# The first layer's bias of a fused attention and gated MLP block: loaded as 14 rows and turned on TensorE instead of by single elements

## The chip, the cores and the metric

One core of a Trainium2 chip runs the kernel. The metric is the device time of one execution in microseconds, of which the median of several runs is taken. Each engine (TensorE or PE, VectorE or DVE, ScalarE or ACT, GpSimd or POOL, and SyncE or SP, which issues the DMAs) works through its own list of instructions in a fixed order.

## What is computed

```python
# x: (1, 2048, 512); 32 query heads of 16, one shared key and value head of 16
xn = _layernorm(x)
q, k, v = xn @ wq, xn @ wk, xn @ wv
s = softmax(q k^T / 4) v  (each head), joined, @ wo
h = xn @ w1 + b1                       # w1: (512, 1792), b1: (1792,)
act = h * tanh(softplus(h))            # Mish
g = silu(act @ w2)                     # w2: (1792, 512)
return x + s * g
```

All inputs and the result are in 32 bits.

## The kernel before

The sequence is cut into four chunks of 512 rows (`C`), the model width into four tiles of 128, and the hidden width of 1792 into `NFT` = 14 tiles of 128. Attention works in 32 units, one for each chunk and group of four heads; a unit is 16 steps of 128 keys. Most products split both operands into a high part (fp32r) and a low part and add three partial products, so for the projection of one weight tile on one chunk TensorE runs 12 matmuls of 128x512 (`mm12`, L649; `Mm`, L104).

Three streams are interleaved on TensorE. Products `m` (L1073) give scores whose row maxima DVE takes (L1077). Products `e` (L1044) give the scores again, turned, with the maximum taken off by two more rows of the operands; ACT takes their exponential (L1049), and `pv` (L1131) multiplies it by the values. All projections (q, both MLP layers, the output) run as groups `xps` in the gaps between (`fill`, `waves`, `unit`).

The kernel is unrolled in full by Python code. In the main part the order on each engine is set by patterns and due times. In the lead-in, some first 90 us, a small planner sets it (the loop at L1428): it keeps a list of tasks for each engine with assumed durations and writes the task that can start first. What stands before that loop (L1284 to L1300) is written out in the order of the code, ahead of every planned instruction of its engine.

The lead-in runs so. SP issues the loads of x in tiles of 128 rows (`load_x`, L221), with the first weight tile of q (`load("wq")`), both tiny weight matrices `wk` and `wv` and the first tile of w1 (`load("ws")`, tile `rawws`) between. TensorE runs 24 products on a zeroed tile (`warm`, L1299). For the first chunk DVE takes the statistics of four tiles (L239, L240) and `ve` (L258); ACT makes `rstd` from it with Ln and Exp (L261, L262), DVE refines it and makes `nbias` (L255), ACT and DVE scale the rows (L211, L287), TensorE turns them (`xp`, L298), ACT copies the high part to `xt` (L307) and DVE the low part (L169). Then follow the first group of q (`xps`, L112), the keys and values (`kp`, L339), the copies `qh`/`ql` and their moves into the query tiles `qt` by DMA (L741), and the first maxima `m`. The same steps follow for chunks 1 to 3, in part on POOL (L287, L273 to L282). TensorE gets extra products on zeros (`keep_warm`, L1384) where the planner sees a gap.

The bias b1 is needed with one hidden column on each partition: `b1c`, 128 partitions x 14, is the bias operand of the ACT instruction that ends each group of the first MLP layer:

```python
bias = b1c[:, ft:ft + 1]
act.activation(hb, ps, AF.Identity, bias=bias)      # L785, the first at 56.5 us
```

Its load is the one line

```python
sp.dma_start(b1c, b1.rearrange("(t p) -> p t", p=P))   # L1292
```

which stands in SP's list behind eight tiles of x, the first tiles of wq and w1, wk and wv, and ahead of the other eight tiles of x. Neighbours in a row of `b1c` lie 512 bytes apart in DRAM, so each of the 1792 elements is a piece of its own of four bytes.

Each engine's list is strict: what waits holds all that stands behind it. The DMAs that SP issues share one set of queues on the 16 DMA engines, and eight completion semaphores are used in turn, so that SP issues a DMA only when the one eight places before has landed.

Of the kernel before, what the change touches and what calls it, by code (L numbers as in the profile page):

```python
# [14 lines left out]
F32 = mybir.dt.float32  # L15
F32R = mybir.dt.float32r
AF = mybir.ActivationFunctionType
# [3 lines left out]
P = 128  # L21
# [9 lines left out]
NFT = F // P  # L31
# [91 lines left out]
def block_kernel(ctx: ExitStack, tc: tile.TileContext, x, wq, wk, wv, wo, w1, b1, w2, out):  # L123
    nc = tc.nc
    cp = ctx.enter_context(tc.tile_pool(name="const", bufs=1))
    sb = ctx.enter_context(tc.tile_pool(name="work", bufs=2))
    ps_e = ctx.enter_context(tc.tile_pool(name="ps_e", bufs=3, space=bass.MemoryType.PSUM))
    ps_m = ctx.enter_context(tc.tile_pool(name="ps_m", bufs=3, space=bass.MemoryType.PSUM))
    ps_v = ctx.enter_context(tc.tile_pool(name="ps_v", bufs=1, space=bass.MemoryType.PSUM))
# [4 lines left out]
    pe, act, dve, pool, sp = nc.tensor, nc.scalar, nc.vector, nc.gpsimd, nc.sync  # L134
# [51 lines left out]
    ident = cp.tile([P, P], F32, name="ident")  # L186
# [15 lines left out]
    b1c = cp.tile([P, NFT], F32, name="b1c")  # L202
# [12 lines left out]
    def new_xt(c):  # L215
        xt_of[c] = sb.tile([P, 2, NDT, C], F32R, tag="xt", name=f"xt{c}", bufs=2)
        return xt_of[c]
# [3 lines left out]
    def load_x(c):  # L221
        for tt in range(4):
            if 4 * c + tt < NPT:
                xin[c, tt] = pts[:, 4 * c + tt]
            else:
                xin[c, tt] = sb.tile([P, D], F32, tag=("y0", "sc")[tt % 2], name=f"xin{c}_{tt}", bufs=1)
            sp.dma_start(xin[c, tt], xr[4 * c + tt])
            if (c, tt) == (1, 0):
                sp.dma_start(wkv[:, 0], wk.rearrange("(t p) n -> p t n", p=P))
                sp.dma_start(wkv[:, 1], wv.rearrange("(t p) n -> p t n", p=P))  # L230
                wk_split()
# [213 lines left out]
    def arrived(tag):  # L445
        k, n = todo[tag]
        if taken(tag, k) or tag == "ws" and k < 12 and k > posted[0] + (4 if lead and now[0] < 50 else 2):
            return False
        return k < n and items[tag][k].step + 1 <= (step[0] if lead else max(step[0], step_of(busy[0])) + 0.3)
# [45 lines left out]
    def load(tag):  # L495
        its = items[tag]
        k, n = todo[tag]
        if tag == "wx" and m1_done.get((NC - 2, NFT - 1)) is None or lead and tag == "wq" and n > 1:
            return
        if n == len(its):  # L500
            return
        it = its[n]
        if taken(tag, n) and (tag != "ws" or kept.get(it.key)):
            return
        if n == k and kept.get(it.key):
            it.tile = home(tag, n)
            sp.dma_start(f(it.tile), kept[it.key])
            it.ready = math.ceil(2 * (sp_at(0.5) + 1.6)) / 2
            todo[tag][:] = n + 1, n + 1
        elif n - k < NRAW[tag] and freed and freed[0] <= step[0] + (0.1 if lead else 0.8):  # L510
            freed.popleft()
            r = sb.tile([P, D], F32, tag="raw", name=f"raw{tag}{n}", bufs=RAWS)
            if len(it.src.shape) == 3:
                sp.dma_start(r.rearrange("p (t n) -> p t n", t=NDT), it.src)
            else:
                sp.dma_start(r, it.src)
            it.raw, it.step = r, (lead["arrive"]() if lead else sp_at(0.45))
            todo[tag][1] += 1
# [770 lines left out]
    load_x(1)  # L1289
    xat.update({t: landed(DMA_US) for t in range(4, 8)})  # L1290
    load("ws")
    sp.dma_start(b1c, b1.rearrange("(t p) -> p t", p=P))  # L1292
    load_x(2)
    load_x(3)
    xat.update({t: landed(DMA_US) for t in range(8, 16)})
# [1 line left out]
    warm = ps_v.tile([P, C], F32, tag="v", name="warm")  # L1297
    for _ in range(NWARM):
        pe.matmul(warm, qts[0][:, 0, 0:P], qts[0][:, 0], start=True, stop=True)  # L1299
    new_xt(0)  # L1300
    used = {"e": [], "v": []}

# [117 lines left out]
    def soon(k, t):  # L1420

        return all(d.end is not None and d.end < t + 2.0 or d.end is None and d.deps and d.eng != "DVE" and all(x.end is not None for x in d.deps)
                   for d in k.deps)
# [4 lines left out]
    while True:  # L1428
# [59 lines left out]
        elif k == "J":  # L1488
            tag = next((g for g in ("wq", "ws", "wb") if not any(soon(k, s) for k in plan["POOL"]) and arrived(g) and busy[0] + E0 < s + (4.5 if g == "ws" else 0.5)), None)
# [194 lines left out]
```

## Time and profile before

| | |
|---|---|
| median of 3 runs | 1571.32 us (1570.73 to 1571.49) |
| the profiled execution's own time | 1572.05 us |
| its span (first to last instruction) | 1570.3 us |
| outside the span | 1.75 us |
| mean granted TensorE clock | 0.997 |
| busy: PE, DVE, ACT, POOL | 1556.2, 1348.8, 1289.8, 635.7 us |
| DMA | 73863 packets, 125.47 MB |

The profile is of one execution. A row of its timeline has the start and the duration in us, the engine, the line, the operation, the tiles written and read, and in brackets how long the engine sat idle before it and what released it. A row by stretches has, for each engine, its busy time and in brackets its instructions, then the granted TensorE clock, the share of the 16 DMA engines that was busy, and GB/s. PE is TensorE's matmuls, PEld its weight loads, SPq a DMA issued by SP.

### The profile page before, as it was taken

Reading aid. Unit: us, or ns where it says so; the run is one execution under the profiler, and the core shown is the slowest. Engines: PE = TensorE matmul, PEld = TensorE weight load, DVE = VectorE, ACT = ScalarE, POOL = GpSimd, SP = SyncE. Lnnn points to the kernel's source line nnn. Section 1 sums busy time; section 2 is a strip of 40 time slices with the busy share of each in tenths; the row PEclk is TensorE's granted clock in tenths of the full one; section 3 lists DMA queues with packets and bytes.
Section 4 is the critical chain, followed back from the end, with each engine's and each line's share of the span. In section 5 each row is a group of like instructions: output and inputs, shape, how many; then the busy total and the mean of one; then the engine's idle time right before and its main releaser. Section 6 shows DMA issues by size and latency. Waiting matters only on the chain.

```text
span 1570.3 us, 31407 instructions
## 1 busy us (share of the span) xinstructions
PE 1556.2 (99%) x11723; PEld 879.3 (56%) x11723; DVE 1348.8 (86%) x2281; ACT 1289.8 (82%) x2501; POOL 635.7 (40%) x668
## 2 busy tenths in 40 slices
PE   9999999999999999999999999999999999999998
PEld 5555655655555565565555556556555555655654
DVE  7998888888988988888998988888889998888844
ACT  5588888789898778977989788897788978888786
POOL 4687448356357202431624422163152323315022
PEclk9999999999999999999999999999999999999999
DMA  6233134133151303203113320322321213031110
GB/s 199 95 128 129 39 103 139 44 112 112 36 162 52 104 21 112 72 19 104 52 51 116 92 92 17 103 67 80 101 59 49 91 57 117 16 98 32 47 49 28
DMA packets 73863, 125.47 MB, mean 80 GB/s; under 512 B 21536, under 2 KB 35136, under 8 KB 73712
## 3 DMA queue, kind: packets, MB, share of 16 engines
q1 hardware_dynamic: 73568, 123.21, 25.3%
q8 instruction: 93, 1.52, 0.4%
q14 instruction: 58, 0.48, 0.1%
q10 hardware_dynamic: 144, 0.26, 0.0%
HBM read 75.57 MB, written 26.21 MB: 65 GB/s over the span
## 4 chain that ended last, share of the span: by engine, by line
PE 95%; ACT 2%; DVE 1%; DMA 1%; issue 0%; POOL 0%; SPq 0%; DVEq 0%; POOLq 0%; ACTq 0%
PE xps L116 43%; PE pv L1131 32%; PE m L1073 12%; PE e L1044 6%; PE xps L112 1%; ACT pts L1049 1%; DVE mb L1077 1%; PE kp L339 0%; DMA pts<-in_dram 0%; PE xp L298 0%; PE wop L116 0%; DMA rawwb<-in_dram 0%; PE warm L1384 0%; PE wop L112 0%; ACT xt L307 0%
## 5 line engine op out<-in xcount | busy, mean ns | idle before, releaser
L1077 DVE TENSOR_REDUCE mb<-m 128x1 f32<-128x512 f32 x2048 | 1266.8, 684 | 170.9 <-PE m L1073 145.4
L1049 ACT ACTIVATE pts<-e 128x512 f32<-128x512 f32 x2038 | 1060.1, 607 | 221.0 <-PE e L1044 152.3
L1073 PE MATMUL m<-ks,qt 48*128 48x512 f32 (+1 forms) x2048 | 842.5, 425 | 0.7 <-DVE mb L1077 0.5
L1044 PE MATMUL e<-qt,ks 64*128 64x512 f32 x2048 | 750.2, 407 | 2.1 <-ACT pts L1049 1.9
L1131 PE MATMUL pv<-pts,vaug 128*32 128x512 f32 x4076 | 530.1, 603 | 0.0
L1073 PEld LDWEIGHTS m<-ks,qt 48*128 48x128 f32 (+1 forms) x2048 | 368.1, 185 | 105.8 <-DVE mb L1077 53.4
L1044 PEld LDWEIGHTS e<-qt,ks 64*128 64x128 f32 x2048 | 373.9, 186 | 26.4 <-ACT pts L1049 12.6
L116 PE MATMUL xps<-wbs,act 64*128 64x512 f32 x1248 | 315.3, 397 | 0.0
L116 PE MATMUL xps<-xt,ws 64*128 64x512 f32 x1128 | 313.0, 410 | 0.4 <-ACT pts L1049 0.3
L116 PEld LDWEIGHTS xps<-xt,ws 64*128 64x128 f32 x1128 | 194.3, 185 | 183.0 <-ACT pts L1049 121.4
L116 PEld LDWEIGHTS xps<-wbs,act 64*128 64x128 f32 x1248 | 226.2, 185 | 65.3 <-ACT pts L1049 32.7
L1131 PEld LDWEIGHTS pv<-pts,vaug 128*32 128x32 f32 x4076 | 88.1, 108 | 151.4 <-issue 143.5
L169 POOL TENSOR_TENSOR hb<-hb,t 128x512 f32<-128x512 f32 x56 | 72.2, 1289 | 167.9 <-ACT t L804 87.7
L179 POOL TENSOR_SCALAR t<-t 128x512 f32<-128x512 f32 x56 | 34.4, 615 | 174.7 <-ACT t L791 174.6
L116 PE MATMUL xps<-xt,wq 64*128 64x512 f32 x336 | 93.1, 410 | 0.0
L116 PEld LDWEIGHTS xps<-xt,wq 64*128 64x128 f32 x336 | 57.9, 185 | 54.8 <-ACT pts L1049 37.7
L169 POOL TENSOR_TENSOR oc<-oc,sc 128x512 f32<-128x512 f32 (+1 forms) x16 | 20.7, 1291 | 153.7 <-DMA qt<-qh 78.6
L116 PE MATMUL xps<-wbs,ot_all 64*128 64x512 f32 x288 | 79.3, 408 | 0.0
L116 PEld LDWEIGHTS xps<-wbs,ot_all 64*128 64x128 f32 x288 | 49.5, 184 | 46.7 <-ACT pts L1049 28.5
L169 POOL TENSOR_TENSOR act<-hb,act 128x512 fp32r<-128x512 f32 x56 | 72.1, 1288 | 4.7
L169 POOL TENSOR_TENSOR hb<-hb,u 128x512 f32<-128x512 f32 x56 | 72.2, 1289 | 4.4
L169 POOL TENSOR_TENSOR u<-u,t 128x512 f32<-128x512 f32 x56 | 71.9, 1285 | 4.7
(154 smaller groups left out, 898.1 us busy)
## 6 DMA issues: line engine op xcount, KB each, us to landing
wbs<-w SPq DMA_DIRECT2D x38, 512.0 KB
ws<-w SPq DMA_DIRECT2D x36, 512.0 KB
qt<-qh SPq DMA_DIRECT2D x256, 32.0 KB
w<-wbs SPq DMA_DIRECT2D x14, 512.0 KB
wq<-wq SPq DMA_DIRECT2D x14, 512.0 KB
wbs<-wo SPq DMA_DIRECT2D x12, 512.0 KB
rawws<-in_dram SPq DMA_DIRECT2D x20, 256.0 KB
w<-ws SPq DMA_DIRECT2D x10, 512.0 KB
```

The source lines that it names most:

```text
L112: self.pe.matmul(ps, self.lhs(), self.rhs(), start=(self.k == 0), stop=(self.k == self.tot - 1))
L116: i = self.pe.matmul(ps, self.lhs()[o], self.rhs()[o], start=(self.k == 0 and self.halves == 0), stop=(self.k == self.tot - 1 and self.hal ...
L169: eng.tensor_tensor(out=o, in0=a, in1=b, op=op)
L179: pool.tensor_scalar(o, o, lim, 0.0, op0=ALU.min, op1=ALU.max)
L1044: pe.matmul(e, ks[o:o + 64, P * k:P * (k + 1)], q[o:o + 64, p], start=True, stop=True)
L1049: x = act.activation(dst, e, AF.Exp, scale=0.25)
L1073: pe.matmul(m, q[o, p, P * t:P * (t + 1)], ks[o, C * kb:C * (kb + 1)], start=True, stop=True)
L1077: return dve.reduce_max(out=mb_of[v][:, kb, z:z + 1], in_=m, axis=AX.X)
L1131: pe.matmul(o[32 * j:32 * j + 32], vaug[:, k], pt, start=(k == 0), stop=(k == 15))
```

## The change

The load of the bias becomes a load of 14 rows of 128 elements, each row contiguous in DRAM, into a tile `b1r` with one row on each of 14 partitions. It stands at the same place in SP's list. Behind the 24 products on zeros, and ahead of all that the planner writes, TensorE turns this tile with one transpose into a PSUM tile `b1t` (128 x 14), and ACT copies that to `b1c`. `b1t` takes the buffer that `warm` had and `kp` takes next.

```diff
     load("ws")
-    sp.dma_start(b1c, b1.rearrange("(t p) -> p t", p=P))
+    b1r = sb.tile([NFT, P], F32, tag="st1", name="b1r", bufs=1)
+    sp.dma_start(b1r, b1.rearrange("(t p) -> t p", p=P))
     load_x(2)
     load_x(3)
...
     for _ in range(NWARM):
         pe.matmul(warm, qts[0][:, 0, 0:P], qts[0][:, 0], start=True, stop=True)
+    b1t = ps_v.tile([P, NFT], F32, tag="v", name="b1t")
+    pe.transpose(b1t, b1r, ident[0:NFT, 0:NFT])
+    act.activation(b1c, b1t, AF.Copy)
     new_xt(0)
```

On TensorE, the start of the list before (`warm` on `qt_79` is the planner's own two products on zeros, `xp` the transposes of x, `xps` the first group of q):

```order
L1299 MATMUL warm<-qt_77 128x512 x24
L1384 MATMUL warm<-qt_79 128x512 x2
L298 MATMUL xp_204<-ident,pts 128x128 x4
L298 MATMUL xp_213<-ident,pts 128x128 x4
L298 MATMUL xp_219<-ident,pts 128x128 x4
L298 MATMUL xp_226<-ident,pts 128x128 x4
```

and the same place of the changed kernel:

```order
L1300 MATMUL warm<-qt_77 128x512 x24
L1302 MATMUL b1t<-ident,b1r 128x14
L1388 MATMUL warm<-qt_79 128x512 x2
L298 MATMUL xp_208<-ident,pts 128x128 x4
L298 MATMUL xp_217<-ident,pts 128x128 x4
L298 MATMUL xp_223<-ident,pts 128x128 x4
L298 MATMUL xp_230<-ident,pts 128x128 x4
```

The transpose of the bias is the 25th instruction of TensorE; nothing else of its list moves, and all of it now stands behind this one.

On ACT, the start of the list before (`rstd` is the first chunk's, `wq` the high part of q's first weight tile, `pts` the scaled rows, `xt` the turned ones):

```order
L1220 ACT_TABLE_LOAD
L261 ACTIVATE rstd<-ve 128x4
L262 ACTIVATE rstd<-rstd 128x4
L467 ACTIVATE wq_193<-rawwq_115 128x512
L211 ACTIVATE pts<-pts,nbias,rstd 128x512 x2
L307 ACTIVATE xt_173<-xp_204 128x4x128
```

and of the changed kernel:

```order
L1220 ACT_TABLE_LOAD
L1303 ACTIVATE b1c<-b1t 128x14
L261 ACTIVATE rstd<-ve 128x4
L262 ACTIVATE rstd<-rstd 128x4
L467 ACTIVATE wq_197<-rawwq_115 128x512
L211 ACTIVATE pts<-pts,nbias,rstd 128x512 x2
L307 ACTIVATE xt_177<-xp_208 128x4x128
```

The copy of the bias is ACT's first computing instruction, ahead of `rstd`. SP, DVE and POOL keep their lists; of SP's only the shape of the one load differs.

## The prediction

> **What bounds the kernel now.** I read the page first, for the engine that sets the pace and for the chain that ended last.
>
> ```profile
> span 1570.3 us, 31407 instructions
> PE 1556.2 (99%) x11723; PEld 879.3 (56%) x11723; DVE 1348.8 (86%) x2281; ACT 1289.8 (82%) x2501; POOL 635.7 (40%) x668
> ...
> PE 95%; ACT 2%; DVE 1%; DMA 1%; issue 0%; POOL 0%; SPq 0%; DVEq 0%; POOLq 0%; ACTq 0%
> ```
>
> TensorE bounds the whole. But the change touches only the first microseconds, where an average says nothing, so the second view is busy time by stretches, for the main part and the two before it.
>
> ```profile
> 90.00:1557.00 1467.00, 1465.20 (x11302) 825.25 (x11302) 1265.88 (x2127) 1237.76 (x2384) 581.51 (x584) 1.00 0.25 76
> 60.00:90.00 30.00, 26.50 (x126) 15.02 (x123) 28.73 (x51) 14.08 (x25) 22.07 (x22) 1.00 0.24 78
> ```
>
> From 90 us on TensorE is busy 1465.2 of 1467 us with an unchanged list. A lead-in that ends later therefore moves this part as a block; nothing in it can give time back. From 60 to 90 us DVE is the busy one, on row maxima whose operands come out of the lead-in, so it moves too. The third view is the chain of waits from the start.
>
> ```profile
> 8.11 0.18 DVE ve L258
> ...
> 8.31 0.21 ACT rstd L261
> ...
> 9.62 1.53 ACT pts L211 x2
> ...
> 11.17 2.07 ACT xt L307 x4
> ...
> 13.29 3.20 PE xps L112 x12
> ...
> 16.51 0.60 ACT qh L723
> ...
> 19.32 0.78 POOL pts L287
> ...
> 20.14 0.66 PE xp L298 x4
> ```
>
> Almost every piece is an engine working on what the last one made, and ACT's `rstd` at 8.31 us is one of them. Whatever delays that instruction delays the rest by as much, unless a later wait is for something else. The timeline shows the places that the change touches.
>
> ```profile
> 7.21 0.43 SPq L514 DMA_DIRECT2D rawws<-in_dram  x1
> ...
> 7.93 0.39 SPq L1292 DMA_DIRECT2D b1c<-in_dram  x1
> ...
> 8.31 0.21 ACT L261 ACTIVATE rstd<-ve 128x4 f32<-128x4 f32 x1 [6.30 <-DVE ve L258]
> ...
> 8.95 2.68 SPq L227 DMA_DIRECT2D pts<-in_dram  x1
> ...
> 9.03 0.61 PE L1384 MATMUL warm<-qt 128*128 128x512 f32 x2
> ...
> 10.38 1.97 PE L298 MATMUL xp<-ident,pts 128*128 128x128 f32 x16 [0.73 <-DVE pts L287]
> ```
>
> The bias is issued at 7.93 us, 0.38 us before `rstd` starts. In the changed order `rstd` stands behind a copy of the turned bias, and TensorE's list waits from 9.03 us, when its 24 products are issued, for the same load.
>
> **When the 14 rows land.** The sizes of the loads and the bytes moved by stretches tell it.
>
> ```profile
> pts<-in_dram SPq DMA_DIRECT2D x14, 256.0 KB
> rawwq<-in_dram SPq DMA_DIRECT2D x2, 256.0 KB
> ...
> wkv<-in_dram SPq DMA_DIRECT2D x2, 32.0 KB
> b1c<-in_dram SPq DMA_DIRECT2D x1, 7.0 KB
> ```
> ```profile
> 0.00:11.00 11.00, 8.28 (x32) 6.48 (x33) 6.45 (x19) 3.60 (x6) 6.37 (x16) 1.00 0.86 240
> 11.00:11.50 0.50, 0.50 (x7) 0.50 (x6) 0.47 (x2) 0.47 (x2) 0.50 (x3) 1.00 0.58 103
> 11.50:12.50 1.00, 1.00 (x10) 0.95 (x9) 0.80 (x3) 1.00 (x3) 1.00 (x6) 1.00 0.43 25
> 12.50:16.00 3.50, 3.26 (x14) 2.17 (x13) 3.43 (x8) 1.25 (x3) 2.53 (x3) 1.00 0.94 287
> ```
>
> Ahead of the bias SP issues eight tiles of x, one tile of wq, one of w1 (as large) and both parts of `wkv`: 10 x 256 KB + 2 x 32 KB = 2.69 MB. The rows give 240 GB/s x 11 us + 103 x 0.5 = 2.69 MB by 11.5 us. So the load ahead has moved its last bytes then, and the bias follows: the stretch of 25 GB/s up to 12.5 us is its 1792 small pieces. The 14 rows are 14 pieces behind the same backlog. They land at 11.5 us at the earliest and, a little after the hole's end, at 13.0 at the latest; I take 12.3, the middle.
>
> **What is added.** TensorE's transpose has one 128-column weight load and a tiny product; ACT copies 128x14. Near rows of the same kinds:
>
> ```profile
> L368 PEld LDWEIGHTS vp<-ident,vt x4: 133/135/138, 23.2 to 23.4; 32*128 32x128 f32 x4
> L368 PE MATMUL vp<-ident,vt x4: 220/222/243, 23.2 to 23.4; 32*128 32x32 f32 x4
> L378 ACT ACTIVATE vaug<-vp x3: 205/223/223, 36.7 to 59.1; 128x64 f32<-128x64 f32 x3
> ```
>
> That is 0.135 + 0.222 = 0.36 us and 0.2 us, with three hand-overs of some 0.03 us (the gap between pieces of the chain, 8.29 to 8.31): 0.6 us. So `rstd` starts at 12.3 + 0.6 = 12.9 instead of 8.31: **+4.6 us** (bounds by the landing 3.8 and 5.3). Nothing covers it. ACT did idle 6.30 us before `rstd`, but that idle time ends at 8.31, before the load can land. Queued behind ACT's wait stand `rstd`, the high part of wq, the scaled rows and all copies; behind TensorE's wait its two products on zeros and the transposes of x, which need ACT's rows anyway and so lose nothing more. POOL's split of wk needs neither and goes on.
>
> **What is removed.** SP's issue of the ninth tile of x takes 2.68 us behind the bias, against 0.43 for `rawws`: 2.25 us earlier for all later loads, and the hole in the traffic goes. Who waits for them? In the next rows DVE, which reads those tiles, is busy 4.65 of 5 us without them being late, and the first maxima wait 0.19 us for a DMA.
>
> ```profile
> 16.00:21.00 5.00, 4.33 (x23) 2.62 (x22) 4.65 (x12) 2.67 (x6) 2.99 (x10) 1.00 1.00 346
> ```
> ```profile
> 22.34 0.47 PE L1073 MATMUL m<-ks,qt 64*128 64x512 f32 x1 [0.19 <-DMA qt<-ql]
> ```
>
> The moves of q are issued later by the whole delay and then find empty queues, so this 0.19 us goes: **-0.2 us**. Between nothing and 2.25 us I take 0.2, the only wait for a DMA on the chain after 6.4 us in this stretch.
>
> **The clock.** The gap on TensorE grows from 0.7 us (before `xp`) to 9.03 to 12.3, and after half a microsecond of work again to `xp` at 10.38 + 4.6 = 15.0. Of 5.9 us only some 0.9 are work. What clock follows such a stretch is seen at the end of the kernel and in the lead-in.
>
> ```profile
> 22.19:25.60 3.41, 3.17 (x15) 1.92 (x16) 2.76 (x6) 3.15 (x12) 1.09 (x6) 1.00 0.31 74
> 25.60:32.43 6.83, 6.83 (x24) 3.20 (x24) 3.51 (x6) 4.52 (x11) 2.87 (x4) 0.50 0.57 188
> 1565.01:1568.42 3.41, 0.62 (x3) 0.19 (x1) 2.02 (x3) 0.00 (x0) 1.29 (x2) 1.00 0.74 275
> 1568.43:1570.30 1.87, 0.00 (x0) 0.00 (x0) 0.00 (x0) 0.00 (x0) 0.00 (x0) 0.50 0.15 57
> ```
>
> The granted clock fell to 0.50 after 3.41 us with 0.62 us of work at the end, and even after 22.19 to 25.60, where half-height products with gaps make 3.17 us; it came back 6.83 us later. So I expect 0.50 before `xp` starts. The products on zeros give the price of it: the rows show 7 begun from 2 to 5 us and 18 from 5.2 to 9, which is 0.43 and 0.21 us each.
>
> ```profile
> L1299 PE MATMUL warm<-qt 128*128 128x512 f32 x7 | 3.3, 646 | 2.0 <-DVE one L191 2.0
> ```
> ```profile
> L1299 PE MATMUL warm<-qt 128*128 128x512 f32 x18 | 4.5, 402 | 0.0
> ```
>
> At half speed the 16 transposes take 3.9 instead of 1.97 us. These first products took full speed after some 3 us of dense work. If 3.4 us bring the clock back, that is at 18.4 at the earliest and, with a stretch that begins 3.4 us late, 21.8: half of 3.4 to 6.8 us is lost, less some 0.5 that ACT's copies hide: 1.2 to 2.9. I take **+1.7 us**, near the lower end, as the backlog is dense. The later fall at 25.6 should come again in its shifted place and cancels.
>
> The Trainium skill, "TensorE: Matmul & The Clock Gate", Part 1, states that the clock halves after at least one idle window of about 3.4 us and returns after a busy one of that length. The end of the trace agrees (0.62 us of work in 3.41), the fall at 25.6 us does not, since TensorE worked through that window. By the page's word "idle", a gap of 3.3 us may just escape, and the sum would be the one without a fall (below).
>
> **Sum.** +4.6 - 0.2 + 1.7 = 6.1, rounded to +6.0 us. Against the profiled execution's own 1572.05 us (span 1570.3) that is 1578.05; that execution is 0.73 us above the median of the runs, 1571.32, so the forecast is 1577.3.
>
> **The rivals.** *The clock holds.* +4.6 - 0.2 = +4.4, 1575.7. For it: the transpose and two products break the gap. Against it: the drop at 25.6 us under more work. 0.24.
>
> *The clock stays low through the keys.* A longer fall also halves `xps` and `kp`; 3.5 us more on the sum, 1580.8. For it: the fall at 25.6 us lasted 6.83 us. 0.12.
>
> *The small load overtakes, not slower.* If 14 pieces need not queue behind the tile of w1, the load costs no more than the first one of the kernel in empty queues:
>
> ```profile
> 0.74 1.81 SPq L227 DMA_DIRECT2D pts<-in_dram  x4
> ...
> 3.47 0.69 DVE L239 BATCH_NORM_STATS2 st<-pts 128x6 f32<-128x512 f32 x1 [1.52 <-DMA pts<-in_dram]
> ```
>
> 3.47 - 0.74 = 2.73 us after issue, 10.7, so `rstd` at 11.3: +3.0. With SP's 2.25 and 0.19 us returned in full it is +0.5, 1571.8; it turns to a gain from a landing before 10.1 on. Against it: x before 9 us moves at the queues' full rate in order, and no wait is for the later tiles. 0.09 for no change, 0.04 for faster.
>
> *The delay is paid, but lost later* in DVE's stretch to 90 us: 1571.3 to 1574.4. Against it: DVE's operands all come out of the delayed chain. Counted in the 0.09.
>
> **The numbers.** The forecast's own case has 0.51 and goes from 1576.3 to 1579.2 (1.2 to 2.9 for the clock, a landing within 0.6 of 12.3). The range goes from the earliest landing without a fall and with some of SP's time returned (+3.0, 1574.3) to the latest with a fall of the upper size (5.3 + 2.9 + 0.5 for a second window = +8.7, 1580.0); it leaves out the overtaking load and most of the long fall. 0.2% is 3.14 us, about what a measurement of this kernel tells from no change: faster 0.04, same 0.09, slower 0.87.
>
> **What would show it.** ACT's copy of the bias idle until some 12.6 us behind PE, `rstd` near 12.9; TensorE's transpose of the bias waiting some 3 us for the DMA; SP's ninth tile issued in 0.4 us and no hole at 11.5 us; granted clock 0.50 somewhere from 12 to 22 us; `qh` near 22.6 instead of 16.51; the stretch from the first `pv` to the end as long as before. A bias landing before 10 us, or `qh` at 21, would make the prediction wrong, as would a main part that is not shifted as a block.

## The result, and the profile after

The changed kernel takes 1578.51 us (median of 6 runs, 1577.17 to 1578.62) against 1570.70 for the kernel before in the same runs (1570.14 to 1571.49): a ratio of 1.0046, 95% interval 1.0035 to 1.0056. It is slower by 0.46%, and slower was the forecast. The 7.8 us are 1.8 more than the forecast's 6.0; the time is only 1.2 us above its 1577.3, because that was counted from 1571.32, the higher median of the first three runs, and it lies in the range of 1574.3 to 1580.0. The profiled execution took 1577.62 us, its span is 1575.8.

The page after shows nothing of the cause: the same chain, the same busy times.

```profile
span 1575.8 us, 31411 instructions
PE 1557.3 (99%) x11724; PEld 881.1 (56%) x11724; DVE 1349.7 (86%) x2281; ACT 1290.4 (82%) x2502; POOL 635.2 (40%) x668
...
PE 95%; ACT 2%; DVE 1%; DMA 1%; issue 0%; POOL 0%; SPq 0%; DVEq 0%; POOLq 0%; ACTq 0%
```

The timeline of the first 24 us of the changed kernel does:

```profile
8.26 0.49 SPq L1293 DMA_DIRECT2D b1r<-in_dram  x1
8.42 0.17 DVE L258 TENSOR_SCALAR ve<-mvs 128x4 f32<-128x4 f32 x1
9.21 2.72 SPq L227 DMA_DIRECT2D pts<-in_dram  x6
...
12.59 0.20 PE L1302 MATMUL b1t<-ident,b1r 14*128 14x14 f32 x1 [2.63 <-DMA b1r<-in_dram]
...
12.72 0.73 PE L1388 MATMUL warm<-qt 128*128 128x512 f32 x2
12.83 0.18 ACT L1303 ACTIVATE b1c<-b1t 128x14 f32<-128x14 f32 x1 [10.82 <-PE b1t L1302]
13.04 0.21 ACT L261 ACTIVATE rstd<-ve 128x4 f32<-128x4 f32 x1
...
14.07 1.26 POOL L169 TENSOR_TENSOR wq<-rawwq,wq 128x512 fp32r<-128x512 f32 x1 [1.86 <-ACT wq L467]
14.10 1.25 DVE L255 SCALAR_TENSOR_TENSOR nbias<-mvs,rstd 128x4 f32<-128x4 f32 x1
...
15.39 1.52 ACT L211 ACTIVATE pts<-pts,nbias,rstd 128x512 f32<-128x512 f32 x2 [1.39 <-DVE nbias L255]
...
15.99 3.67 PE L298 MATMUL xp<-ident,pts 128*128 128x128 f32 x16 [2.54 <-DVE pts L287]
...
20.91 3.04 PE L112 MATMUL xps<-xt,wq 128*128 128x512 f32 x12
...
23.99 0.60 ACT L723 ACTIVATE qh<-xps 128x512 fp32r<-128x512 f32 x1 [3.17 <-PE xps L112]
```

`ve`, the operand of `rstd`, is ready at 8.59 us. ACT touches it at 13.04, because its first instruction waits for TensorE's transpose, and that for the load. From there the delay grows step by step. The start of a span against its work moves by some tenths from one execution to the next (`ve` is ready at 8.28 us in the profile before), so single differences of this table are no better than that. Start times, in us:

| | before | after | late by |
|---|---|---|---|
| `rstd` | 8.31 | 13.04 | 4.73 |
| scaled rows `pts` on ACT | 9.62 | 15.39 | 5.77 |
| transposes `xp` | 10.38 | 15.99 | 5.61 |
| first group of q, `xps` | 13.29 | 20.91 | 7.62 |
| `qh` | 16.51 | 23.99 | 7.48 |
| first maximum `m` | 22.34 | 29.54 | 7.20 |
| first `pv` of the chain | 91.45 | 96.29 | 4.84 |
| end of the span | 1570.3 | 1575.8 | 5.5 |

The first maximum of the changed kernel:

```profile
29.54 0.96 PE L1073 MATMUL m<-ks,qt 64*128 64x512 f32 x3
```

Two steps of this table need rows of their own. Between `rstd` and `pts`, `nbias` took 1.25 us, to the end of POOL's subtraction; before it took 0.20:

```profile
9.38 0.20 DVE L255 SCALAR_TENSOR_TENSOR nbias<-mvs,rstd 128x4 f32<-128x4 f32 x1
```

Between `xp` and `xps` the granted clock (the number after POOL's column) was half. The stretches of the changed kernel:

```profile
10.18:13.59 3.41, 0.86 (x3) 0.43 (x3) 0.08 (x1) 0.71 (x4) 2.03 (x10) 1.00 0.93 303
13.59:17.01 3.42, 1.02 (x5) 1.02 (x6) 3.26 (x7) 1.93 (x3) 1.26 (x1) 0.50 1.04 374
17.01:20.42 3.41, 3.41 (x16) 3.11 (x14) 2.35 (x5) 2.51 (x5) 0.00 (x0) 0.50 0.22 82
20.42:25.60 5.18, 5.03 (x22) 3.39 (x21) 4.65 (x11) 1.29 (x4) 1.89 (x4) 1.00 0.18 51
25.60:32.43 6.83, 6.07 (x33) 3.92 (x32) 5.05 (x11) 5.62 (x15) 3.15 (x11) 1.00 0.27 61
```

It fell at 13.59, after a stretch with 0.86 us of work on TensorE, and came back at 20.42, after one that was full. The last row is where the kernel before had its own fall to 0.50: here it did not come, and some 2.5 us of the 7.2 were given back (7.20 late at the first maximum, 4.65 late at the 17th). What the change was for did happen: SP's six issues of x follow at once (2.72 us in all, where one of them alone had taken 2.68), and the hole in the traffic is filled.

```profile
11.00:11.50 0.50, 0.00 (x0) 0.00 (x0) 0.00 (x0) 0.00 (x0) 0.50 (x3) 1.00 0.95 312
11.50:12.50 1.00, 0.00 (x0) 0.00 (x0) 0.00 (x0) 0.00 (x0) 0.71 (x4) 1.00 0.91 314
```

The same rows show what it cost: in this time PE, DVE and ACT have no work.

### The profile page after: what moved, and what is told of

It is laid out like the page before. It is cut to its first block, busy times and chain, and to the rows that moved or that the text cites. A ratio compares the mean times of both kernels' runs of the same rounds, so it can differ in the third digit from the quotient of the medians.

```text
span 1575.8 us, 31411 instructions
## 1 busy us (share of the span) xinstructions
PE 1557.3 (99%) x11724; PEld 881.1 (56%) x11724; DVE 1349.7 (86%) x2281; ACT 1290.4 (82%) x2502; POOL 635.2 (40%) x668
## 4 chain that ended last, share of the span: by engine, by line
PE 95%; ACT 2%; DVE 1%; DMA 1%; issue 0%; POOL 0%; SPq 0%; DVEq 0%; POOLq 0%; ACTq 0%
PE xps L116 43%; PE pv L1131 32%; PE m L1073 12%; PE e L1044 6%; PE xps L112 1%; ACT pts L1049 1%; DVE mb L1077 1%; PE xp L298 0%; DMA rawwq<-in_dram 0%; PE kp L339 0%; DMA b1r<-in_dram 0%; DMA rawwb<-in_dram 0%; PE wop L116 0%; PE warm L1388 0%; PE wop L112 0%
```

## The experiments

The first theory: the loss is the wait for the load at the head of ACT's list, and what the delayed start brings on (POOL's hold on `nbias`, the clock). Its rivals: TensorE's wait or the added instructions are the loss; the new form of the load is; the removed pieces are worth something that the wait hides. Each kernel is compared with the kernel before on the same chip, whose median stands beside it.

**The changed kernel again.** No edit.

> The changed kernel as it is, once more, beside the others on one chip. First theory (the wait for the 14 rows holds ACT and TensorE, 4.7 us, and what the clock and POOL add to it comes on top): 6 to 8 us over the kernel before, the first maximum (m) some 7 us late, and the granted clock 0.50 once between 12 and 22 us. Where the time is above 1578 rather than near 1577.4, the clock should fall a second time between 25 and 40 us, as it does in the kernel before. Rival (these two levels are two chips and have nothing to do with the clock): the same number of falls in both.

Measured: 1577.75 us against 1570.73, ratio 1.0038 (1.0026 to 1.0050). `rstd` at 12.51 us, `nbias` 1.25 us, one early fall of the clock (13.9 to 20.7), first maximum at 29.29. The profiled execution (1576.54 us) had no second fall. Of the other four only the mean granted clock is known: one has 0.998 and took 1577.23 us, three have 0.997 and took 1577.75 to 1579.08. The longer ones have the lower clock, but rounded means do not tell whether a second fall makes it. From the first start of a product `pv` to the end it took 1478.87 us, as the kernel before (1478.88); the 1479.59 of the first profile were that execution's own.

**The turn written later.** The 14-row load stays, transpose and copy stand ahead of the first group of q (the lines are those that differ from the changed kernel):

```diff
-    b1t = ps_v.tile([P, NFT], F32, tag="v", name="b1t")
-    pe.transpose(b1t, b1r, ident[0:NFT, 0:NFT])
-    act.activation(b1c, b1t, AF.Copy)
     new_xt(0)
...
                 xt_done[0] = step[0]
+                b1t = ps_v.tile([P, NFT], F32, tag="v", name="b1t")
+                pe.transpose(b1t, b1r, ident[0:NFT, 0:NFT])
+                act.activation(b1c, b1t, AF.Copy)
                 fill(12)
```

> The load of 14 rows stays; transpose and copy stand behind the transposes of x, ahead of the first group of q, where the rows have long landed. First theory (only the wait in front costs): rstd at 8.3 us again, no gap on TensorE, the time of the kernel before within 0.5 us. Rival (the transpose, the copy or the 14-row load cost in themselves): 2 us or more of the loss stay. Second rival (the removed 1792 pieces were worth something): 1 to 2.5 us faster than before.

Measured: 1569.91 us against 1570.73, ratio 0.9992 (0.9984 to 1.0001). ACT's rows:

```profile
7.87 0.20 ACT L261 ACTIVATE rstd<-ve 128x4 f32<-128x4 f32 x1 [5.85 <-DVE ve L258]
...
12.84 0.18 ACT L1343 ACTIVATE b1c<-b1t 128x14 f32<-128x14 f32 x1
```

`rstd` waits for `ve` again, and the copy runs without a wait of its own. The whole loss is gone with the same load, the same transpose and the same copy: they cost nothing in this place that these times could show, and the rival of their own cost falls. For a hidden gain the interval leaves room up to 0.16%, that of the repeat below (0.9990 to 1.0009) up to 0.10%, or 1.6 us. The rows leave less: from `rstd` to the first maximum it takes 13.81 us here and 14.03 before.

**No load at all.** The kernel before, with `b1c` filled with zeros, so that the bias is left out.

```diff
-    sp.dma_start(b1c, b1.rearrange("(t p) -> p t", p=P))
+    pool.memset(b1c, 0.0)
```

> The kernel before without any load of the bias: b1c is filled with zeros by POOL, so the bias is left out of the result. It shows at most what the removal of the 1792 pieces can bring. First theory (no engine on the chain waits for the loads behind them, but for 0.2 us): 0 to 0.5 us faster, the first maximum at most 0.3 us earlier. Rival (SP's 2.68 us and the hole in the traffic are paid by the lead-in): 1.5 to 2.5 us faster.

Measured: 1570.21 us against 1570.73, ratio 0.9994 (0.9985 to 1.0002). The traffic has no hole, and the first maximum starts where it did:

```profile
11.50:12.50 1.00, 1.00 (x12) 1.00 (x11) 0.78 (x3) 1.00 (x3) 1.00 (x6) 1.00 1.09 394
```
```profile
22.32 0.96 PE L1073 MATMUL m<-ks,qt 64*128 64x512 f32 x3
```

The same maximum began at 22.34 before. Counted from `rstd` (8.57 here, 8.31 before) it comes 13.75 us later instead of 14.03, and no longer waits for a DMA. So the 1792 pieces, all of them, were worth some 0.3 us up to there in this execution, and over the whole, by the interval, at most 0.15%: the loads behind them were early anyway.

**The load issued early.** The 14 rows go out as the fifth DMA, the transpose stands behind 19 of the 24 products on zeros.

```diff
     load_x(0)
+    b1r = sb.tile([NFT, P], F32, tag="st1", name="b1r", bufs=1)
+    sp.dma_start(b1r, b1.rearrange("(t p) -> t p", p=P))
...
-    sp.dma_start(b1c, b1.rearrange("(t p) -> p t", p=P))
...
-    for _ in range(NWARM):
+    for k in range(NWARM):
+        if k == 19:
+            b1t = ps_m.tile([P, NFT], F32, tag="m", name="b1t")
+            pe.transpose(b1t, b1r, ident[0:NFT, 0:NFT])
+            act.activation(b1c, b1t, AF.Copy)
         pe.matmul(warm, qts[0][:, 0, 0:P], qts[0][:, 0], start=True, stop=True)
```

> The load of 14 rows is issued as the fifth DMA, right behind the first four tiles of x, and the transpose stands behind 19 of the 24 products on zeros; the copy stays ACT's first instruction, ahead of rstd. First theory: the rows land near 7 us, ACT's copy is done by 8.2 us and the loss is gone, up to the 0.5 us by which one more issue of SP delays the later loads: within 0.5 us of before. Rival (a copy ahead of rstd and a transpose in the lead-in cost wherever the rows come from): 2 us or more slower than before.

Measured: 1572.61 us against 1570.73, ratio 1.0007 (0.9998 to 1.0015). The ratio is not to be told from 1, but the median is 1.9 us higher, so neither the 0.5 us of the theory nor the 2 us of the rival is settled by this run. The forecast time of the copy was missed: the 19 products took to 8.46 us, and ACT was free of the copy at 8.94 while `ve` had been there since 7.1. The wait had moved from the DMA to TensorE's list. The run "Early load, early turn" below settles it.

**TensorE's wait alone.** Only ACT's copy moves, to where the late turn has it; the transpose stays in front.

```diff
     pe.transpose(b1t, b1r, ident[0:NFT, 0:NFT])
-    act.activation(b1c, b1t, AF.Copy)
...
                 xt_done[0] = step[0]
+                act.activation(b1c, b1t, AF.Copy)
                 fill(12)
```

> The transpose stays in front on TensorE; only ACT's copy moves behind the copies of the turned x. It parts TensorE's wait from ACT's. First theory (each engine's wait delays the chain by itself): rstd at 8.3 us and nbias unhindered, but the transposes of x start behind the rows and the two products on zeros, near 13.3 instead of 10.4 us, the clock falls as in the changed kernel; 3 to 5 us over before, some 2.5 us less than the changed kernel (1.7 by the earlier start, 1 by POOL). Rival (ACT's wait alone is the loss): within 0.5 us of before. Second rival (TensorE's wait alone is the loss): as slow as the changed kernel.

Measured: 1574.13 us against 1570.02, ratio 1.0026 (1.0015 to 1.0038). TensorE's rows:

```profile
12.47 0.20 PE L1302 MATMUL b1t<-ident,b1r 14*128 14x14 f32 x1 [2.26 <-POOL wk L169]
12.61 0.73 PE L1388 MATMUL warm<-qt 128*128 128x512 f32 x2
13.18 1.91 PE L298 MATMUL xp<-ident,pts 128*128 128x128 f32 x16
```

The transpose reads `ident`, made in the first two microseconds, and `b1r`, so the wait that the row puts down to POOL is taken to be the load's (in the repeat, where POOL ended `wk` at 11.5 us, the transpose waited to 12.07, and its row names the DMA). The scaled rows were ready from 10 us on (`rstd` at 8.19), but the transposes began at 13.18, 2.8 us later than before. The work is dense behind the gap, and the clock did not fall in this execution, where I expected it to; it took 1572.31 us, 2.3 over the median before. It was one of the shorter ones: five of the other six have a mean clock of 0.998 or 0.996 and took 1573.66 to 1576.24 us, so the 4.1 us between the medians hold falls of the clock that this profile does not show. TensorE's wait costs by itself too, and is the shorter of two waits for one load.

**ACT's wait alone, with the old load.** The kernel before, and one copy of `b1c` into an unread tile as ACT's first instruction.

```diff
+    b1w = sb.tile([P, NFT], F32, tag="st1", name="b1w", bufs=1)
+    act.activation(b1w, b1c, AF.Copy)
     for _ in range(NWARM):
```

> The kernel before with its load of 1792 pieces, and one ACT copy of b1c, into a tile that nobody reads, as ACT's first instruction. It has the wait on ACT and nothing else of the change: TensorE's list is that of before. First theory (what costs is that ACT waits for this load ahead of rstd, whatever form the load has): rstd near 13.1 us (the old load lands a little later), 6 to 8 us slower than before, nbias held by POOL as well. Rival (TensorE's wait or the transpose is the greater part): 3 us or less.

Measured: 1577.21 us against 1569.82, ratio 1.0046 (1.0032 to 1.0060), the changed kernel's very ratio.

```profile
12.64 0.21 ACT L1299 ACTIVATE b1w<-b1c 128x14 f32<-128x14 f32 x1 [10.62 <-DMA b1c<-in_dram]
12.76 0.19 ACT L261 ACTIVATE rstd<-ve 128x4 f32<-128x4 f32 x1
```

With no transpose and no new load, the wait on ACT alone makes the loss, with the same hold on `nbias` (1.26 us) and the same fall of the clock (13.4 to 20.2). The 1792 pieces landed about when the 14 rows do: both stand behind the same 2.69 MB.

**TensorE kept busy through the wait.** 38 products on zeros ahead of the transpose and 8 behind.

```diff
-NWARM = 24
+NWARM = 38
...
     act.activation(b1c, b1t, AF.Copy)
+    w2 = ps_m.tile([P, C], F32, tag="m", name="warm2")
+    for _ in range(8):
+        pe.matmul(w2, qts[0][:, 0, 0:P], qts[0][:, 0], start=True, stop=True)
```

> The changed kernel with 38 instead of 24 products on zeros ahead of the transpose and 8 more behind it, so that TensorE works through the wait. Theory (part of the loss is the clock that falls in the gap): no 0.50 between 12 and 22 us, the transposes of x take 2.0 instead of 3.7 us, qh is 1.5 to 2 us earlier than in the changed kernel; the whole 1 to 2 us faster than it if nothing else moves. Rival (the clock in the lead-in costs nothing, since ACT and DVE set the pace there): the changed kernel's time within 0.4 us.

Measured: 1575.63 us against 1570.02, ratio 1.0034 (1.0021 to 1.0047). The clock stayed at 1.00, and its mean is 1.000 in all five executions:

```profile
10.20:13.60 3.40, 3.29 (x15) 2.45 (x14) 0.00 (x0) 0.20 (x2) 1.94 (x9) 1.00 1.00 329
13.60:20.40 6.80, 5.81 (x33) 4.36 (x31) 5.96 (x12) 4.89 (x10) 1.67 (x2) 1.00 0.61 209
```
```profile
13.14 0.20 PE L1302 MATMUL b1t<-ident,b1r 14*128 14x14 f32 x1
...
16.57 1.97 PE L298 MATMUL xp<-ident,pts 128*128 128x128 f32 x16 [0.74 <-DVE pts L287]
18.29 0.94 PE L1391 MATMUL warm<-qt 128*128 128x512 f32 x3
19.48 3.19 PE L112 MATMUL xps<-xt,wq 128*128 128x512 f32 x12 [0.25 <-ACT xt L307]
```

From the first transpose to `xps` it takes 2.91 us as before, against 4.92 in the changed kernel: the clock costs 2.0 us there. Not all of it is won: the 38 products last to 13.0 us, so the transpose, at 13.14, waits for them and no longer for the load, and `rstd` starts at 13.58, 0.54 us later than in the changed kernel. `qh` comes at 22.71, 1.28 us earlier, less than expected. Over the whole the two ratios (1.0034, and 1.0038 of the repeat) overlap, so the gain is shown by the rows and only suggested by the times (5.6 and 7.0 us over their own kernels before; the slowest of the five executions, 1575.99, is below the fastest of the eleven of the changed kernel, 1576.54).

**The gap without the wait.** The kernel before with half the products on zeros.

```diff
-NWARM = 24
+NWARM = 12
```

> The kernel before with 12 instead of 24 products on zeros: TensorE stops near 6 us and has nothing to do up to the transposes of x at 10.4 us. It has the gap of the changed kernel without its wait. Theory: the clock falls to 0.50 from some 10 us on, the transposes of x and perhaps the first group of q run at half speed, and the first maximum comes 1 to 3 us late; the whole 0.5 to 3 us slower than before. Rival (the gap alone does not lower the clock, or it costs nothing): the time of before within 0.4 us.

Measured: 1571.79 us against 1570.02, ratio 1.0008 (0.9999 to 1.0018). The clock fell, for half as long:

```profile
7.80:11.20 3.40, 1.35 (x11) 1.03 (x10) 2.69 (x9) 2.67 (x6) 2.08 (x8) 0.99 1.10 290
11.20:14.60 3.40, 3.25 (x13) 2.46 (x12) 3.06 (x6) 2.58 (x5) 2.75 (x7) 0.51 0.73 193
```

The transposes took 2.78 instead of 1.97 us and `qh` came at 17.54. A gap alone can bring the fall, in this execution at least; one of the eleven has a mean clock of 1.000. From `rstd` to the first maximum it took 14.93 us instead of 14.03; the price over the whole is not told apart from nothing here.

**POOL's subtraction in quarters.** The changed kernel, with POOL's 128x512 subtraction for `wq` cut into four of 128x128. In the first try each quarter was charged to the planner as a whole subtraction, the planner then wrote another order, and the kernel took 1591.67 us (ratio 1.0137); of it only the duration of `nbias` counts, 0.45 us.

```diff
-        sub(pool, w[:, 1], it.raw, f(w[:, 0]))
+        for o in ([slice(128 * n, 128 * n + 128) for n in range(4)] if it.key == ("q", 0) and lead else [slice(0, D)]):
+            sub(pool, w[:, 1, o], it.raw[:, o], f(w[:, 0, o]))
```

> The changed kernel, with POOL's one subtraction for the low part of q's first weight tile (128x512, 1.26 us) cut into four of 128x128. In the changed kernel DVE's nbias (128x4) took 1.25 us, from 14.10 to the very end of that subtraction, and 0.20 us before. Theory (DVE's instruction is held until POOL's is through): nbias takes 0.5 us or less, the scaled rows start 0.7 to 1 us earlier, the whole 0.5 to 1 us faster than the changed kernel. Rival (nbias waits for something else that ends at the same time, such as ACT): 1.2 us again and no change.

In the second try they are charged as one, and every other instruction stands as in the changed kernel:

```diff
-        sub(pool, w[:, 1], it.raw, f(w[:, 0]))
+        if it.key == ("q", 0) and lead:
+            charge(1.3)
+            for o in (slice(128 * n, 128 * n + 128) for n in range(4)):
+                pool.tensor_tensor(out=w[:, 1, o], in0=it.raw[:, o], in1=f(w[:, 0, o]), op=ALU.subtract)
+        else:
+            sub(pool, w[:, 1], it.raw, f(w[:, 0]))
```

> The four quarters of POOL's subtraction again, now charged to the planner as one, so that every other instruction stands where it does in the changed kernel. Theory (DVE's nbias is held until POOL's instruction is through): nbias takes 0.45 us as with the quarters before, not 1.25; the scaled rows start 1.3 us after nbias' start is reached at the earliest in the changed kernel and 0.5 us here; the first maximum and the whole 0.6 to 0.9 us earlier than in the changed kernel, some 1577. Rival (the longer work of POOL, 2.06 against 1.26 us, comes due later): no gain in the whole, or a loss.

Measured: 1576.17 us against 1569.82, ratio 1.0039 (1.0025 to 1.0053).

```profile
13.35 2.06 POOL L473 TENSOR_TENSOR wq<-rawwq,wq 128x128 fp32r<-128x128 f32 x4 [2.06 <-ACT wq L467]
13.38 0.44 DVE L255 SCALAR_TENSOR_TENSOR nbias<-mvs,rstd 128x4 f32<-128x4 f32 x1
13.86 1.52 ACT L211 ACTIVATE pts<-pts,nbias,rstd 128x512 f32<-128x512 f32 x2 [0.58 <-DVE nbias L255]
```

`nbias` follows the length of POOL's instruction, 0.44 us with quarters and 1.25 with the whole: it is held until that one is through. Of the 0.8 us won there, 0.5 was left at `xps` (7.35 us behind `rstd`, against 7.87 in the changed kernel) and 0.16 at the first maximum (16.34 against 16.50). `xps` began at 19.66 us, still at half clock (to 20.5 here), where that of the changed kernel began after the clock was back: the clock took some 0.4 us of the gain. Where the rest went is not shown, and against the repeat's 1.0038 the time of the whole shows no gain.

**Early load, early turn.** The early load with the transpose behind 12 products on zeros instead of 19, to undo the miss above.

```diff
-        if k == 19:
+        if k == 12:
```

> The 14 rows as the fifth DMA, and the transpose behind 12 instead of 19 products on zeros, so that ACT's copy is over before ve. Theory: rstd starts 0.03 us behind ve again, no part of the change is waited for, the time of before or of the late turn within 0.4 us. Rival (a fifth load ahead of the other tiles delays them by its 0.5 us of issue and the lead-in with them): 0.5 us or more slower.

Measured: 1570.56 us against 1569.82, ratio 1.0005 (0.9996 to 1.0014).

```profile
6.85 0.18 ACT L1303 ACTIVATE b1c<-b1t 128x14 f32<-128x14 f32 x1 [4.84 <-PE b1t L1302]
...
7.27 0.17 DVE L258 TENSOR_SCALAR ve<-mvs 128x4 f32<-128x4 f32 x1
...
7.47 0.21 ACT L261 ACTIVATE rstd<-ve 128x4 f32<-128x4 f32 x1 [0.44 <-DVE ve L258]
```

The same copy stands at the same place of ACT's list as in the changed kernel, and now costs nothing, because its load lands before `ve`.

**The late turn again.** The same kernel as above.

> The late turn (14 rows loaded, transposed and copied ahead of the first group of q) once more, against before on the same chip, to see whether its lead of 0.08% holds. First theory: between the time of before and 1 us less. Rival (the removed pieces bring what SP waits, 2.25 us): 1.5 us less or more.

Measured: 1569.66 us against 1569.82, ratio 0.9999 (0.9990 to 1.0009). The lead of 0.08% did not hold; the late turn is the same as the kernel before. Its two profiled executions differ by one fall of the clock, which only the second one had (26.60 to 30.02 us):

```profile
26.60:30.02 3.42, 3.42 (x23) 1.52 (x21) 2.30 (x5) 3.06 (x8) 0.87 (x2) 1.00 0.50 164
```
```profile
26.60:30.02 3.42, 3.42 (x15) 1.78 (x14) 1.10 (x2) 2.33 (x7) 0.79 (x2) 0.51 0.35 108
```

From the first maximum to the 17th it took 12.39 us without the fall and 13.88 with it; in the kernel before, whose fall lasted twice as long, 14.90. One kernel with one list of instructions shows both.

## Why the prediction came out as it did

**The landing and the wait: right.** Forecast 12.3 us for the landing and +4.6 at `rstd`; the transpose began at 12.59 (12.07 in the repeat, 12.47 with the copy late) and `rstd` was 4.73 late. Counted from `ve`, whose start moves with the execution, `rstd` lost 4.42 us, and 4.76 in the repeat. The late turn, the early load and the old load with a wait show that it is this wait, and nothing that the change adds or removes otherwise.

**"Queued behind TensorE's wait ... lose nothing more": right in the changed kernel,** where ACT's rows come later still. TensorE's wait alone costs 2.8 us at the transposes, but there it is hidden behind ACT's.

**What is removed, -0.2 us: borne out by the rows.** Without the load the first maximum comes 0.28 us sooner behind `rstd`, and its wait of 0.19 us for a DMA is gone. The ratio, 0.9994 (0.9985 to 1.0002), fits this, but cannot tell 0.2 us from nothing or from 2.

**The clock in the gap: right, and near in size.** Forecast +1.7 us; 2.0 between `xp` and `xps`.

**Not in the sum: DVE held by POOL, +1.05 us.** The prediction took the pieces between `rstd` and the scaled rows to keep their lengths. POOL "goes on", it says, and that was the step that missed: because POOL had finished splitting wk by 12.2 us, its subtraction for `wq` waited only for ACT's high part of `wq`, which stands right behind `rstd` (13.38 to 13.99 us), and so came due just when `nbias` did. Before, that high part was ready at 9.28, but POOL was at wk until it began the subtraction at 12.46, long after `nbias`. This and the 0.3 us more of clock are most of why `qh` came at 23.99 us and not near the 22.6 that was forecast.

**"The later fall at 25.6 should come again in its shifted place and cancels": wrong.** It is a matter of the execution, not of the kernel: the profiled execution before had it (and was 0.73 us above its median), those of the changed kernel did not. So the profiled difference, 1577.62 - 1572.05 = 5.57 us, holds some 2.5 us of clock to the new kernel's credit, and the medians, 1578.51 - 1570.70 = 7.8, do not. The lateness at the first maximum comes out of the table as 4.73 (wait) + 1.04 (DVE) - 0.16 + 2.01 (clock) - 0.42 (given back from `xps` to `m`, the 0.19 us of the DMA among it) = 7.20; the forecast's 6.0 lacks the 1.04 of DVE.

The mean granted clock, which is known for each execution of the experiments and of the changed kernel, bears this out. Over 1570 us a fall of 6.83 us takes 0.0022 off the mean, one of 3.41 half of that, and the one at the end, which lasted at most 2.33 us in the 14 profiles, up to 0.0007. The kernel before ran 66 times beside the experiments. In 33 executions the mean is 1.000, so that there was no fall but at the end; they have a median of 1570.02 us (1569.18 to 1571.55). In six it is 0.997, for which a fall of 3.41 us and the end are too little; they took 1572.04 to 1573.04. The profiled one, 0.997 and 1572.05, is of the second kind; the six times of the comparison, 1570.14 to 1571.49, lie with the first. Of the six executions of the changed kernel the one with 0.998 (1577.17 us) has room for the early fall alone, and two with 0.996 (1578.53 and 1578.62) need a longer or a further one. So a later fall, or a longer early one, comes in the changed kernel too, in some executions, and raises the median. What the change costs where neither kernel has a later fall is best seen beside the repeat: its two executions with 0.998 took 1576.54 and 1577.23 us, the kernel before with 1.000 a median of 1570.48, so 6.1 to 6.8 us. The profile of the late turn, which has no later fall either, lies near: its first `pv` started at 88.83 us, that of the changed kernel at 96.22, 7.39 later, or 6.63 counted from `ve`.

## What to carry to other kernels

A small load was here as late as the loads ahead of it in the queue, and cutting its pieces did not make it early. An instruction that only prepares an operand for much later belongs behind the instructions of its engine that are on the chain, or its load ahead of theirs: here the first use was at 56.5 us, and the place in ACT's list turned a copy of 0.18 us into 4.7. And a wait at the start is not shifted work alone: look at what then falls together (DVE and POOL) and at the gap on TensorE that lowers its clock. Where the clock falls in some executions only, compare executions with the same mean clock before a difference of a few microseconds is put down to the kernel.

## What the runs showed of the hardware that was not expected

DVE's `nbias` (128x4, two operands in SBUF) took 0.20 us beside POOL's short instructions, 1.25 beside one of 1.26 us and 0.44 beside the first of four quarters. The Trainium skill, "SBUF — State Buffer", section "SBUF: two separate sides", says that a DVE instruction with two SBUF inputs and a GpSimd instruction that reads SBUF share a pair of ports, and that whichever starts first keeps it for its whole length. The three numbers agree.

The clock fell after a stretch of 3.41 us in which TensorE had still worked 0.86 us (changed kernel) and after one of 3.40 with 1.35 (fewer products on zeros), so a gap need not be empty for it. With a gap of 2.3 us and dense work behind it (the copy late), it did not fall in the profiled execution; in five of the other six it fell somewhere, as their means of 0.998 and 0.996 show. It stayed at 0.50 for 3.4 us or 6.8 us, and one and the same kernel ran with a later fall and without (the kernel before at 0.997 and at 1.000).
